# Two token steps of a 2048-point transform on 64 by 64 tiles of the PE array, and W fetched two groups at a time

## The chip, the cores and the metric

The kernel runs on one core of a Trainium2 chip. The metric is device time in microseconds. A profile is of one execution; its span runs from the first instruction to the last, and that execution's own time is a little longer. Engines are written as the profile writes them: PE (TensorE; PEld is its weight load), DVE (VectorE), ACT (ScalarE), POOL (GpSimd) and SP (SyncE, which only issues DMA transfers).

## What is computed

x is 2048 tokens by 1024 channels. Two branches read it, and a gate mixes them.

```
a = irfft2( rfft2(x) * (w_r + i w_i) )             # over tokens and channels; w: 2048 x 513
Lam_bar = exp(exp(log_dt) * Lambda)
B_bar   = ((Lam_bar - 1) / Lambda)[:, None] * (B_re + i B_im)
h[t]    = Lam_bar * h[t-1] + x[t] @ B_bar.T        # 1024 complex states, 2048 tokens in order
b       = 2 * Re(h @ (C_re + i C_im).T) + x * Dskip
g       = sigmoid(sum(x * gate_w, -1))
out     = g * a + (1 - g) * b
```

## The kernel before, in words

**The spectral branch (`gfnet`).** The 2048-point transform over tokens is split as 64 x 32. The first stretch, "the front", works in 16 row blocks j. `turn_x(j)` turns a block of x on PE (L684) and ACT copies it out (L685). `fold(j)` forms sums and differences on DVE (L695 to L701). `fd(j)` is the transform over channels, eight matmuls (L359, L362) copied to X1 by ACT or DVE (L365). `s1(j)` is the first token step with the twiddles T2: four matmuls of 64 rows each (L376), copied to A1 by DVE for j in 0, 1, 2, 3, 5, 6, 7, else by ACT (L381), then written to DRAM (L383). In the second stretch, 16 groups g of two rows b follow. `load(g)` brings Bb back turned (L408) and W, real and imaginary, each into both partition halves, in four transfers (L411). `s2(g)` is the second token step: two matmuls of 128x128 against the constant KRS (L488), which ACT copies to X2 (L490). `times_w(g)` makes the products X2 * w_i and X2 * w_r on DVE (L496, L497). The first inverse step, `ps_is1`, is four matmuls of 128x128 against the twiddles MT (L512, L513), copied to C1 by ACT (L515) and written to DRAM (L516). The third stretch reads that back turned (L530) and does the second inverse step in 16 blocks of sixteen 128x128 matmuls (L537), copied to ZT by ACT (L539). The inverse over channels is `spectral(tb)` (L629), per token tile.

Column 512 of W has no room in the half spectrum, so a small side path computes its products: `reverse_m`, `zps`, `qps` (L410 to L484). Its result Qn is put into column 0 of each X2 (L491).

**The state branch.** Tokens go in 8 chunks of 256. `unit(c, q)` makes the inputs of chunk c: two halves of 32 matmuls (L319), each copied to h by ACT (L321). `recur(c, ...)` then cuts the recurrence into DVE pieces: multiplications by a rotation table ("cross" and "along", L274, L277), joins (L280, L283), scans of 1024 columns each, four for a whole chunk (L289), a carry, and the rotation back. The table itself is made by `make_tab` in the front, in five parts per pair of blocks on DVE, ACT and POOL (L226 to L248, and L856 to L863). `early(tb)` is the output product of a token tile, two halves of 16 + 4 matmuls (L598, L602), for tiles 0 to 9; tiles 10 to 15 are done at the end. It waits for the pieces of its chunk. `load_C` and `load_xs` are DMA transposes (L583, L590) and write CT and xs.

**What sets the order.** The order on PE, DVE and ACT is that of the program (`manual_schedule`); the order on SP and POOL is chosen by the framework's own planner. In the front, `plan[j]` gives the order of turn (T), fold (f), `fd(j+1)` (F) and `s1(j)` (S); from j = 6 on the main loop places parts of the table, halves of the state branch and loads around it. `step()` advances the spectral branch by one stage, `halves(ssm, 1)` the state branch by one half. `vector(us)` takes DVE pieces off the list until their nominal costs reach the sum of the shares given so far; the shares are the numbers in SHARE, one per call. In the second stretch each group is: s2(g+2), ps_is1(g), times_w(g+1), loads for g+3, one half of the state branch, one share.

**Buffers that matter.** PSUM pool psA has two buffers, shared in turn by fd, s1, s2 and both inverse steps. Bb and W have three buffers each, V2 and C1 two. `raw` is 6144 columns wide: T2 takes its first half in the front, MT all of it in the second stretch, and the third stretch reads its blocks into it.

Of the kernel before, what the change touches and what calls it, by code (L numbers as in the profile page):

```python
# [32 lines left out]
    4, 5.2, 3.6, 5.9, 2.8, 1, 1, 2.2, 2.2, 3.7, 2.2, 3, 3, 3, 2.5, 3.5,  # L33
    3, 2.2, 3.3, 3.3, 4.8, 3.3, 3.3, 3.3, 3.3, 3.3, 3, 2.6, 3, 3.3, 3.3, 3.3,
    2.5, 3, 3.2, 3, 0, 2, 4, 2, 2, 2, 2.5, 2, 2, 1.5, 2, 2,
    2, 2, 2, 2, 3.5, 3.5, 3.5, 4, 6, 4, 4, 2, 4, 4, 4.5, 4.5,
    4.5, 4.5, 4.5, 4.8, 4.3, 4.3, 4.3,
# [8 lines left out]
def _host_consts():  # L46
# [14 lines left out]
    for cls in range(2):  # L61
        for kb in range(2):
# [10 lines left out]
    m1 = np.arange(64)[None, None, :]  # L73
# [20 lines left out]
    gr, gb, ga = f // 64, (f // 2) % 32, f % 2
    angR = 2 * np.pi * ((gb[:, None] * gb[None, :]) % 32) / 32
    R2 = (ga[:, None] == ga[None, :]) * np.where(gr[:, None] == gr[None, :], np.cos(angR),
                                                  np.where(gr[:, None] == 0, 1.0, -1.0) * np.sin(angR))
    R2 = R2.reshape(P, 64, 2).transpose(0, 2, 1).reshape(P, P)
    Sel = np.zeros((P, 2, 2, P))
    for h in range(2):  # L100
        for ri in range(2):
            Sel[2 * np.arange(64) + h, h, ri, 64 * ri + np.arange(64)] = 1.0
# [18 lines left out]
def kernel(  # L121
# [29 lines left out]
    W_v = [w.rearrange("(p b) k -> p b k", b=32) for w in (A_w_r, A_w_i)]  # L151
# [197 lines left out]
    def gfnet():  # L349
# [4 lines left out]
        def fd(j):  # L354
# [9 lines left out]
            X1 = gta.tile([P, 2, K], BF16, name="X1")  # L364
# [5 lines left out]
        def s1(j):  # L370
# [10 lines left out]
            (nc.vector.tensor_copy if j in (0, 1, 2, 3, 5, 6, 7) else nc.scalar.copy)(out=A1, in_=psa)  # L381
# [14 lines left out]
        MT_sb = raw.rearrange("p (b n) -> p b n", n=192)  # L396
# [5 lines left out]
        t1_v = turn1_dram.rearrange("j (r a b) k -> (j r a) b k", r=2, a=2)  # L402
        Wb = fft["Wb"]

        def load(g):
            bs = slice(2 * g, 2 * g + 2)
            Bb = gt.tile([P, 2, K], BF16, name="Bb", tag="gin", bufs=3)
            nc.sync.dma_start(out=Bb, in_=t1_v[:, bs])  # L408
            for w in range(2):
                for r in range(2):  # L410
                    nc.sync.dma_start(out=Wb[g % 3][64 * r:64 * (r + 1), w, :, 1:K], in_=W_v[w][:, bs, 1:K])  # L411
            return Bb

# [22 lines left out]
        loads = [load(0), load(1), load(2)]  # L436
# [4 lines left out]
        nc.vector.tensor_copy(out=Bcol[:, 0:2].rearrange("j c a b -> j (c a b)"), in_=aps)  # L441
# [64 lines left out]
        for g in range(16):  # L506
# [13 lines left out]
            if g + 3 < 16:  # L520
                loads.append(load(g + 3))
# [343 lines left out]
    for _ in range(5):  # L865
        front()
# [145 lines left out]
```

## Time and profile before

| | before |
|---|---|
| median of 3 runs | 339.19 us (338.52 to 339.42) |
| the profiled execution: time | 338.71 us |
| the profiled execution: span | 336.9 us |
| mean granted PE clock | 0.995 |
| PE, DVE, ACT, POOL busy | 323.7, 286.7, 169.3, 32.4 us |
| moved by DMA | 58.45 MB, 173 GB/s over the span |

In rows of the timeline a group of neighbouring equal instructions is one line: start, length, engine, line of the code, operation, output <- inputs, shapes and count; in square brackets stands the idle time of the engine before it and what ended that. A matmul's length reaches past the start of the next one, so PE work is read from start to start. SPq rows are the issuing of transfers, not the transfers.

### The profile page before, as it was taken

Reading aid. Unit: us, or ns where it says so; the run is one execution under the profiler, and the core shown is the slowest. Engines: PE = TensorE matmul, PEld = TensorE weight load, DVE = VectorE, ACT = ScalarE, POOL = GpSimd, SP = SyncE. Lnnn points to the kernel's source line nnn. Section 1 sums busy time; section 2 is a strip of 40 time slices with the busy share of each in tenths; the row PEclk is TensorE's granted clock in tenths of the full one; section 3 lists DMA queues with packets and bytes.
Section 4 is the critical chain, followed back from the end, with each engine's and each line's share of the span. In section 5 each row is a group of like instructions: output and inputs, shape, how many; then the busy total and the mean of one; then the engine's idle time right before and its main releaser. Section 6 shows DMA issues by size and latency. Waiting matters only on the chain.

```text
span 336.9 us, 6192 instructions
## 1 busy us (share of the span) xinstructions
PE 323.7 (96%) x2446; PEld 213.7 (63%) x2446; DVE 286.7 (85%) x403; ACT 169.3 (50%) x213; POOL 32.4 (10%) x64
## 2 busy tenths in 40 slices
PE   8998859999999999999999999999999999999995
PEld 4564636676885675747566576869845876565552
DVE  2798895899979789999999999899680999999951
ACT  3888679746351155647556551646632243443510
POOL 1481112020000000000000000000000002211220
PEclk9999989999999999999999999999999999999999
DMA  7999999999992447889999956997214003776594
GB/s 265 378 175 227 204 211 208 164 172 218 272 220 55 115 135 175 251 192 284 261 253 252 232 163 170 216 195 203 70 28 136 19 0 53 109 159 89 98 156 154
DMA packets 83581, 58.45 MB, mean 173 GB/s; under 512 B 54328, under 2 KB 74304, under 8 KB 83424
## 3 DMA queue, kind: packets, MB, share of 16 engines
q1 hardware_dynamic: 80304, 55.38, 66.8%
q0 software_dynamic: 3168, 2.66, 8.7%
q8 instruction: 19, 0.31, 0.4%
q14 instruction: 10, 0.08, 0.1%
q10 hardware_dynamic: 80, 0.01, 0.0%
HBM read 30.23 MB, written 17.83 MB: 143 GB/s over the span
## 4 chain that ended last, share of the span: by engine, by line
PE 83%; ACT 5%; DVE 5%; SPq 4%; issue 1%; DMA 1%; ACTq 0%; DVEq 0%
PE ps_y L598 29%; PE psu L319 28%; PE ps_h L598 4%; PE ps_id L629 4%; SPq L583 3%; PE ps_fd L359 2%; PE ps_is L537 2%; PE ps_is L513 2%; PE ps_is L512 2%; PE ps_s L488 2%; PE ps_y L602 2%; PE pt L684 2%; PE psw L710 1%; ACT xQ L685 1%; SPq L411 1%
## 5 line engine op out<-in xcount | busy, mean ns | idle before, releaser
L319 PE MATMUL psu<-xQ,BT 128*128 128x256 bf16 x1024 | 117.9, 275 | 0.8 <-ACT ye L616 0.5
L319 PEld LDWEIGHTS <-BT 128*128 128x128 bf16 x1024 | 100.1, 99 | 17.4 <-issue 3.2
L598 PE MATMUL ps_y<-CT,h 128*128 128x512 bf16 x448 | 101.3, 379 | 0.0
L598 PEld LDWEIGHTS <-h 128*128 128x128 bf16 x512 | 49.4, 98 | 55.4
L289 DVE TENSOR_TENSOR_SCAN h<-rz,h 128x1024 bf16<-128x1024 f32 x32 | 71.5, 2274 | 0.1
L321 ACT CAST h<-psu 128x1024 bf16<-128x1024 f32 x32 | 32.3, 1010 | 52.5 <-PE psu L319 49.2
L277 DVE TENSOR_TENSOR h<-h,tab 128x4096 bf16<-128x4096 bf16 (+1 forms) x20 | 37.3, 1863 | 0.7
L644 POOL DMA_DIRECT2D BT<-y_scratch x10 | 11.9, 1194 | 235.4 <-DVE BT L638 235.1
L616 ACT ACTIVATE ye<-ps_y,omg 128x512 f32<-128x512 f32 x20 | 12.7, 684 | 43.4 <-PE ps_y L602 35.7
L274 DVE TENSOR_TENSOR xQ<-h,tab 128x4096 bf16<-128x4096 bf16 x12 | 27.4, 2287 | 4.4 <-ACT h L321 4.3
L490 ACT CAST X<-ps_s 128x1024 bf16<-128x1024 f32 x16 | 16.2, 1014 | 8.7 <-PE ps_s L488 8.7
L359 PE MATMUL ps_fd<-G_sb,preT 128*128 128x512 bf16 x64 | 16.5, 380 | 1.2 <-ACT X L365 1.2
L685 ACT COPY xQ<-pt 128x1024 bf16<-128x1024 bf16 x16 | 15.4, 1024 | 2.5 <-PE pt L684 2.5
L539 ACT CAST ZT<-ps_is 128x1024 bf16<-128x1024 f32 x16 | 15.5, 1023 | 2.2 <-PE ps_is L537 2.2
L695 DVE TENSOR_TENSOR preT<-xQ 128x512 bf16<-128x512 bf16 x16 | 7.3, 453 | 10.9 <-ACT xQ L685 7.6
L515 ACT CAST C<-ps_is 128x1024 bf16<-128x1024 f32 x16 | 16.1, 1008 | 0.0
L629 PE MATMUL ps_id<-raw,ZT 128*128 128x256 bf16 x128 | 15.9, 273 | 0.0
L365 ACT CAST X<-ps_fd 128x1024 bf16<-128x1024 f32 x14 | 14.2, 1013 | 3.0 <-PE ps_fd L362 2.9
L376 PE MATMUL ps_s<-X,raw 64*128 64x512 bf16 x64 | 9.7, 380 | 5.1 <-DVE CT L381 4.5
L598 PE MATMUL ps_h<-CT,h 128*128 128x512 bf16 x64 | 14.5, 379 | 0.0
L629 PEld LDWEIGHTS <-ZT 128*128 128x128 bf16 x128 | 12.4, 98 | 2.2
L496 DVE TENSOR_TENSOR V<-X,Wb 128x1024 bf16<-128x1024 bf16 x16 | 10.9, 680 | 1.6 <-issue 1.5
(194 smaller groups left out, 367.9 us busy)
## 6 DMA issues: line engine op xcount, KB each, us to landing
y_scratch<-ye SPq DMA_DIRECT2D x20, 256.0 KB, 2.6
CT<-in_A_x_dram SPq DMA_DIRECT2D x8, 512.0 KB, 5.4
Bb<-turn_scratch SPq DMA_DIRECT2D x16, 256.0 KB, 4.0
turn_scratch<-C SPq DMA_DIRECT2D x16, 256.0 KB, 5.1
raw<-turn_scratch SPq DMA_DIRECT2D x16, 256.0 KB, 4.5
Wb<-in_A_w_r_dram SPq DMA_DIRECT2D x32, 127.8 KB, 4.1
Wb<-in_A_w_i_dram SPq DMA_DIRECT2D x32, 127.8 KB, 3.8
out_dram<-BT SPq DMA_DIRECT2D x14, 256.0 KB, 5.2
```

The source lines that it names most:

```text
L274: nc.vector.tensor_mul(out=tmps["s"], in0=u[:, ::-1], in1=bc(i))
L277: nc.vector.tensor_mul(out=u, in0=u, in1=bc(i))
L289: nc.vector.tensor_tensor_scan(out=seg, data0=rz[:, js.start + j:js.start + j + 4].rearrange("p j t -> p (j t)"), data1=seg, initial=0.0, ...
L319: nc.tensor.matmul(psu[:, j, :], lhsT=BT[4 * q + j][:, ri, d8, :], rhs=xQ[:, c, d8, :], start=(d8 == 0), stop=(d8 == 7))
L321: nc.scalar.copy(out=hs[c][:, ri, 4 * q:4 * q + 4].rearrange("p b (q j) -> p b q j", j=32), in_=psu.rearrange("p b (j q) -> p b q j", j=32))
L359: nc.tensor.matmul(ps[:, 1, :], lhsT=preTs[j][:, 4 + d4, :], rhs=Go[:, d4, :], start=(d4 == 0), stop=(d4 == 3))
L490: nc.scalar.copy(out=X2, in_=ps2)
L515: nc.scalar.copy(out=C1.rearrange("p h (c i) -> p h c i", c=2), in_=psc.rearrange("p h (i c) -> p h c i", c=2))
L539: nc.scalar.copy(out=ZT[:, 4 * kp:4 * kp + 4, :, 8 * G:8 * G + 8].rearrange("p (c r) n t -> p c r n t", c=2), in_=psz.rearrange("p c (t r ...
L598: nc.tensor.matmul(psy, lhsT=hs[c][:, ri, jb, P * tq:P * (tq + 1)], rhs=CT[ri][:, jb, 512 * dh:512 * (dh + 1)], start=(i == 0), stop=False)
L629: nc.tensor.matmul(pse[:, slot, :], lhsT=ZT_t[:, i, tb, :], rhs=fft["Gi"][:, i, :], start=(kb == 0), stop=(kb == 1))
L685: nc.scalar.copy(out=x_gjq[:, :, :, :, j, :].rearrange("p c d g q -> p d c g q"), in_=pt.rearrange("p d (c q g) -> p d c g q", c=NCH, g=2))
```

## The change

**The tiles.** The frequency order that s1 leaves, and all constants behind it, are permuted so that the second token step couples 64 rows with 64 rows: KRS's first part becomes two copies of a 64 x 64 matrix, and the twiddles MT need 96 columns a row instead of 192. `s2(g)` is then four matmuls of 64x64x512 with `tile_position` (64b, 64c), and `ps_is1(g)` eight, in two rounds that add up in PSUM. The row half of a tile goes with the PSUM bank it writes. The inverse over tokens is thereby split 32 then 64, before 64 then 32; the second inverse step keeps its number and size of matmuls, and its block of input comes in one transfer instead of two. The matmuls of `qps` are four of 32 columns instead of four of 16, and Qn is made by four copies instead of one.

**The fetch.** W sits in two double buffers, each for two groups, one of them partly in the half of `raw` that MT no longer takes. `load_W(i)` brings one of w_r and w_i for two groups in four transfers of 32 partitions by 4 rows. Each partition quarter takes the rows that its 32 frequencies need. Bb has a fourth buffer, also in `raw`. Four groups are loaded ahead instead of three, and each turn of the loop asks for group g+4.

**The order.** `plan` and the loops that stood around it are replaced by one string, ORDER, one letter per act: T, f, F, S as above, h a half of the state branch, v a share, t a part of the table, a a part of the small vectors, b one load of B, c one load of C, s a step of the spectral branch, x the change of PSUM pools, and so on (`acts`). X1 has four buffers instead of two. The A1 copies of s1(2) go to ACT, those of s1(4) and s1(15) to DVE. Written in one notation (S8 is s1(8), u01a the first half of unit(0,1), t4 the fifth part of the tables), the part of the front around s1(8) is

```
before: t0 f10 F7 S6 b b t1 t2 u00a t3 t4 f11 f12 F8 S7 b b t5 t6 u00b t7 t8 F9 f13 S8
after:  t0 f10 F7 b t1 t2 S6 b t3 t4 f11 u00a f12 F8 t5 b b S7 u00b t6 t7 F9 t8 f13 S8
```

The order of halves and of spectral stages in the second and third stretch is the same as before; shares fall at other places and have other sizes. The diff, without most of the constants and without the moved small-vector lines:

```diff
 SHARE = (
-    4, 5.2, 3.6, 5.9, 2.8, 1, 1, 2.2, 2.2, 3.7, 2.2, 3, 3, 3, 2.5, 3.5,
-    3, 2.2, 3.3, 3.3, 4.8, 3.3, 3.3, 3.3, 3.3, 3.3, 3, 2.6, 3, 3.3, 3.3, 3.3,
-    2.5, 3, 3.2, 3, 0, 2, 4, 2, 2, 2, 2.5, 2, 2, 1.5, 2, 2,
-    2, 2, 2, 2, 3.5, 3.5, 3.5, 4, 6, 4, 4, 2, 4, 4, 4.5, 4.5,
-    4.5, 4.5, 4.5, 4.8, 4.3, 4.3, 4.3,
+    4.9, 4.3, 2.1, 5.9, 1.3, 2.5, 3.5, 0.6, 2.5, 4, 2.5, 4.2, 1.5, 3, 2.5, 3.5,
+    4.3, 2.2, 3.3, 2.3, 4.8, 3.3, 2.3, 3.3, 5.3, 1.7, 3, 3.2, 3, 2.7, 2.3, 1.8,
+    2.9, 3, 5.3, 4, 0, 3.5, 4, 1, 2, 2, 3.6, 2.4, 1.4, 3, 0.8, 0.2,
+    2, 2, 3.5, 1.7, 3.8, 6, 3.2, 2.5, 4.5, 4, 3.7, 2.3, 4.3, 4.3, 5.7, 3.7,
+    3.9, 4.5, 2.7, 8.4, 5.8, 4.3, 4,
+)
+ORDER = (
+    "TFfSTfTFTfTbbSbbFTTfSTTbFbfTfSTbbwFTTfb2STbfFaSabbxaatfFbttSbttf",
+    "hfFtbbShttFtfSthSttthfFtttvFSktttthtvgfFSttchvtFStctthFvScttttth",
+    "tvFtStttvtcSvtt|cccsvhcvhvhdvehshvshvhvvshhvshvsshvsshvsshvsshvs",
+    "shvsshsshvvsshvsshvsshvsshvsshsvshvsshvsshvsshvsshvhvhvsvshvsvsh",
+    "vsvshvsshvvsvshsvshvsvivshvsvshv",
 )
 
...
+    K2 = cs(f % 2, h // 32, 2 * np.pi * (((f // 2) * (h % 32)) % 32) / 32)
+    K2 = np.concatenate([K2, K2], axis=1)
+    angM = 2 * np.pi * (((64 * (f % 32) + 32 * (f // 64) + gb) * np.arange(32)[None, None, :]) % S) / S
+    Mre = np.where((f // 32) % 2 == 0, np.cos(angM), -np.sin(angM))
+    Mim = np.where((f // 32) % 2 == 0, np.sin(angM), np.cos(angM))
...
-    W_v = [w.rearrange("(p b) k -> p b k", b=32) for w in (A_w_r, A_w_i)]
+    W_v = [w.rearrange("(m c b) k -> c m b k", c=2, b=32) for w in (A_w_r, A_w_i)]
...
-            X1 = gta.tile([P, 2, K], BF16, name="X1")
+            X1 = gta.tile([P, 2, K], BF16, name="X1", bufs=4)
...
-            (nc.vector.tensor_copy if j in (0, 1, 2, 3, 5, 6, 7) else nc.scalar.copy)(out=A1, in_=psa)
+            (nc.vector.tensor_copy if j in (0, 1, 3, 4, 5, 6, 7, 15) else nc.scalar.copy)(out=A1, in_=psa)
...
-        MT_sb = raw.rearrange("p (b n) -> p b n", n=192)
+        MT_sb = raw[:, 0:3 * D].rearrange("p (b n) -> p b n", n=96)
...
-        t1_v = turn1_dram.rearrange("j (r a b) k -> (j r a) b k", r=2, a=2)
+        t1_v = turn1_dram.rearrange("j (r g b c) k -> g b (j r) c k", r=2, g=16, b=2)
         Wb = fft["Wb"]
 
         def load(g):
-            bs = slice(2 * g, 2 * g + 2)
-            Bb = gt.tile([P, 2, K], BF16, name="Bb", tag="gin", bufs=3)
-            nc.sync.dma_start(out=Bb, in_=t1_v[:, bs])
-            for w in range(2):
-                for r in range(2):
-                    nc.sync.dma_start(out=Wb[g % 3][64 * r:64 * (r + 1), w, :, 1:K], in_=W_v[w][:, bs, 1:K])
+            Bb = (gt.tile([P, 2, K], BF16, name="Bb", tag="gin", bufs=3) if g % 4 < 3
+                  else raw[:, 5 * D:6 * D].rearrange("p (c k) -> p c k", c=2))
+            nc.sync.dma_start(out=Bb, in_=t1_v[g])
             return Bb
+
+        def load_W(i):
+            pair, w = i // 2, i % 2
+            for q in range(4):
+                nc.sync.dma_start(out=Wb[pair % 2][w][32 * q:32 * (q + 1), :, 1:K], in_=W_v[w][q // 2][:, 4 * pair:4 * pair + 4, 1:K])
...
-        loads = [load(0), load(1), load(2)]
+        loads = [load(g) for g in range(4)]
+        for i in range(4):
+            load_W(i)
...
-        qps = psA.tile([P, 2, 16], FP32, name="qps", tag="ps")
-        for h in range(2):
-            for ri in range(2):
-                nc.tensor.matmul(qps[:, h, :], lhsT=fft["Sel"][:, 2 * h + ri, :], rhs=Qb[:, :, ri],
-                                 start=(ri == 0), stop=(ri == 1))
+        qps = psA.tile([P, 4, 32], FP32, name="qps", tag="ps")
+        for a4 in range(4):
+            nc.tensor.matmul(qps[:, a4, :], lhsT=fft["Sel"][:, a4, :], rhs=Qb.rearrange("p b r -> p (b r)"), start=True, stop=True)
         Qn = fx.tile([P, 2, 16], BF16, name="Qn")
-        nc.vector.tensor_copy(out=Qn, in_=qps)
-        Qn = Qn.rearrange("p h b -> p (h b)")
+        for q in range(4):
+            at = slice(32 * q, 32 * (q + 1))
+            nc.vector.tensor_copy(out=Qn[at], in_=qps[at, 2 * (q // 2):2 * (q // 2) + 2, q % 2:32:2])
+        Qn = Qn.rearrange("p a b -> p (a b)")
 
         def s2(g):
             ps2 = psA.tile([P, 2, K], FP32, name="ps_s2", tag="ps")
-            for h in range(2):
-                nc.tensor.matmul(ps2[:, h, :], lhsT=KRS_sb[:, 0, :], rhs=loads[g][:, h, :], start=True, stop=True)
+            for b in range(2):
+                for c in range(2):
+                    nc.tensor.matmul(ps2[64 * c:64 * (c + 1), b, :], lhsT=KRS_sb[64 * b:64 * (b + 1), 0, 0:64],
+                                     rhs=loads[g][64 * b:64 * (b + 1), c, :], start=True, stop=True, tile_position=(64 * b, 64 * c))
...
-            nc.vector.tensor_mul(out=V2, in0=X2, in1=Wb[g % 3][:, 1])
-            nc.vector.tensor_mul(out=X2, in0=X2, in1=Wb[g % 3][:, 0])
+            nc.vector.tensor_mul(out=V2, in0=X2, in1=Wb[g // 2 % 2][1][:, 2 * (g % 2):2 * (g % 2) + 2])
+            nc.vector.tensor_mul(out=X2, in0=X2, in1=Wb[g // 2 % 2][0][:, 2 * (g % 2):2 * (g % 2) + 2])
...
             psc = psA.tile([P, 2, K], FP32, name="ps_is1", tag="ps")
-            for h in range(2):
-                b = 2 * g + h
-                nc.tensor.matmul(psc[:, h, :], lhsT=MT_sb[:, b, 64:192], rhs=UV[0][:, h, :], start=True, stop=False)
-                nc.tensor.matmul(psc[:, h, :], lhsT=MT_sb[:, b, 0:128], rhs=UV[1][:, h, :], start=False, stop=True)
+            for u, n in ((0, 32), (1, 0)):
+                for b in range(2):
+                    for c in range(2):
+                        rows = slice(64 * c, 64 * (c + 1))
+                        nc.tensor.matmul(psc[64 * b:64 * (b + 1), c, :], lhsT=MT_sb[rows, 2 * g + b, n:n + 64], rhs=UV[u][rows, b, :],
+                                         start=(u == 0), stop=(u == 1), tile_position=(64 * c, 64 * b))
...
-            if g + 3 < 16:
-                loads.append(load(g + 3))
+            if g + 4 < 16:
+                loads.append(load(g + 4))
+                load_W(g + 4)
...
-        ZT = fft["ZT"].rearrange("p i t (h u) -> p i (t h) u", h=2)
-        t2_v = turn2_dram.rearrange("b (r G a g) k -> G r b a g k", r=2, a=2, g=4)
+        ZT = fft["ZT"].rearrange("p i t (h u) -> p i (t h) u", h=4)
+        t2_v = turn2_dram.rearrange("b (y G g) k -> G (b y) g k", y=4, g=4)
 
         for G in range(8):
             Cq = raw[:, 2 * D * (G % 3):2 * D * (G % 3 + 1)].rearrange("p (g k) -> p g k", g=4)
-            for r in range(2):
-                nc.sync.dma_start(out=Cq[64 * r:64 * (r + 1)], in_=t2_v[G, r])
+            nc.sync.dma_start(out=Cq, in_=t2_v[G])
             for kp in range(2):
                 psz = psA.tile([P, 2, K], FP32, name="ps_is2", tag="ps")
                 for kl in range(2):
                     kc = 2 * kp + kl
-                    pv = psz[:, kl, :].rearrange("p (a g n) -> p a g n", a=2, g=4)
                     for g in range(4):
-                        nc.tensor.matmul(pv[:, :, g, :], lhsT=Cq[:, g, P * kc:P * (kc + 1)], rhs=KRS_sb[:, 1, :],
+                        nc.tensor.matmul(psz[:, kl, P * g:P * (g + 1)], lhsT=Cq[:, g, P * kc:P * (kc + 1)], rhs=KRS_sb[:, 1, :],
                                          start=True, stop=True)
-                nc.scalar.copy(out=ZT[:, 4 * kp:4 * kp + 4, :, 8 * G:8 * G + 8].rearrange("p (c r) n t -> p c r n t", c=2),
-                               in_=psz.rearrange("p c (t r n) -> p c r n t", t=8, r=2))
+                nc.scalar.copy(out=ZT[:, 4 * kp:4 * kp + 4, :, 4 * G:4 * G + 4].rearrange("p (c r) n g -> p c r n g", c=2),
+                               in_=psz.rearrange("p c (g r n) -> p c r n g", g=4, r=2))
...
-        fft["Wb"] = [fft["wp"].tile([P, 2, 2, K], BF16, name=f"Wb{i}") for i in range(3)]
+        halves_of_W = [fft["wp"].tile([P, 4, K], BF16, name=f"Wb{i}") for i in range(3)]
+        halves_of_W.append(raw[:, 3 * D:5 * D].rearrange("p (x k) -> p x k", k=K))
+        fft["Wb"] = [halves_of_W[0:2], halves_of_W[2:4]]
...
+    def small():
+        nc.vector.tensor_copy(out=ang2[:, 0], in_=thp)
+        nc.vector.tensor_scalar_mul(out=ang2[:, 1], in0=thp, scalar1=float(TC))
+        yield from sincos(sp, ang2, [P, 2, 8], s2c, c2c, "a2")
...
+    def turn(r):
+        turn_x(r)
+        turns_left[0] -= 1
+
+    def use_psU():
+        assert not turns_left[0]
+        xctx.close()
+        pools["u"] = ctx.enter_context(tc.tile_pool(name="psU", bufs=2, space=PSUM, reuse_waits="tile"))
+
+    def front_done():
+        for _ in tables:
+            pass
+        tctx.close()
+
+    def make_dgD():
+        nc.vector.tensor_mul(out=fft["dgD"], in0=ident.unsqueeze(1).to_broadcast([P, 8, P]),
+                             in1=vecT[:, 3].unsqueeze(2).to_broadcast([P, 8, P]))
+
+    acts = {
+        "T": in_turn(turn, 2), "f": in_turn(fold, 2), "F": in_turn(fft["fd"], 1), "S": in_turn(fft["s1"], 0),
+        "h": lambda: halves(ssm, 1), "v": lambda: vector(next(share)), "t": lambda: next(tables, None),
+        "a": lambda: next(smalls, None), "x": use_psU, "g": gate, "b": lambda: load_B(1), "c": in_turn(lambda q: load_C(q - 8), 8),
+        "2": lambda: load_T2(8, 16), "w": load_Wcols, "k": load_small, "|": front_done,
+        "s": step, "d": make_dgD, "e": gate_end, "i": after_ic,
+    }
+    for act in "".join(ORDER):
+        acts[act]()
```

## The prediction, made before the change was run

> **What bounds the kernel now.** I read, in this order, the page's busy shares, the table by stage, the PE timeline of the stage that the change rebuilds, the PE timeline of the front, and then the DVE and SP timelines beside both.
>
> ```profile
> PE 323.7 (96%) x2446; PEld 213.7 (63%) x2446; DVE 286.7 (85%) x403; ACT 169.3 (50%) x213; POOL 32.4 (10%) x64
> ...
> 31.30:52.70 21.40, 16.88 (x127) 12.07 (x128) 19.18 (x59) 15.09 (x27) 3.90 (x6) 0.92 1.11 220
> ...
> 122.70:200.80 78.10, 78.10 (x514) 48.78 (x513) 75.51 (x70) 45.55 (x64) 0.00 (x0) 1.00 0.90 229
> ```
>
> The columns of the last two are the stretch, its length, then PE, PEld, DVE, ACT and POOL busy, the granted clock, the DMA share and GB/s. PE is idle for only 13.2 us of the 336.9 us span. From 122.7 to 200.8 (second token step and first inverse step, with SSM work between the groups) it is never idle, so every PE microsecond taken out there shortens the span until another engine takes over. DVE is the candidate: 75.5 of 78.1.
>
> ```profile
> 137.03 0.59 PE L488 MATMUL ps_s<-Bb,KRS_sb 128*128 128x512 bf16 x2
> 137.47 0.38 PE L512 MATMUL ps_is<-X,raw 128*128 128x512 bf16 x1
> 137.68 0.38 PE L513 MATMUL ps_is<-V,raw 128*128 128x512 bf16 x1
> ...
> 138.33 3.66 PE L319 MATMUL psu<-xQ,BT 128*128 128x256 bf16 x32
> ```
>
> This is one of 16 groups on PE. Read starts, not durations, because matmuls overlap: a 512-column matmul starts 0.215 us after the one before, and the six take 137.03 to 138.33, **1.30 us**.
>
> **Step 1, the blocks.** In the change a group has twelve matmuls of 64 rows by 64 columns, four at a time on disjoint quarters of the array. Does PE run such tiles together? Two nearest rows:
>
> ```profile
> 30.77 0.60 PE L362 MATMUL ps_fd<-G_sb,preT 128*128 128x256 bf16 x4
> 31.31 0.61 PE L376 MATMUL ps_s<-X,raw 64*128 64x512 bf16 x4
> 31.85 3.67 PE L319 MATMUL psu<-xQ,BT 128*128 128x256 bf16 x32
> ...
> 59.93 3.66 PE L319 MATMUL psu<-xQ,BT 128*128 128x256 bf16 x32
> 63.52 1.91 PE L737 MATMUL zps_g<-xQ,gw 128*32 128x512 bf16 x32
> 65.36 1.04 PE L359 MATMUL ps_fd<-G_sb,preT 128*128 128x512 bf16 x4
> ```
>
> L376 splits the rows in two: four matmuls take 0.54 us, where full ones take 0.86. That is 2 x 0.215 + 0.11; and L362 before it takes 0.54 instead of the 0.44 it takes ahead of a full matmul. So the tiles run in pairs, and a visit to the tiled form costs about 0.2 us. L737 splits the columns in four, each with a stream of its own: 32 matmuls in 1.84 us = 8 x 0.215 + 0.12, and the psu ahead of it takes 3.59 instead of 3.50. Again four at once and 0.2 per visit. Rows and columns split together do not occur in this trace. I take the same rule: 3 x 0.215 + 0.2 = 0.845 us a group, saving 0.455. Bounds: 0.755 if one half of the switch is hidden; 1.57 if each matmul with its load needs 114 ns (twice the 57 ns of an L737 pair, for twice its columns).
> Groups 0 to 13: 14 x 0.455 = 6.4. The first two s2 alone: 0.87 becomes 0.63, 0.24. Groups 14 and 15 have no s2: 0.87 and 0.86 become 0.63, 0.47. Sum **7.1 us off PE**. The later inverse step keeps its 128 matmuls of 128x128 (0.89 us a block): nothing.
>
> The weight side: L448 gets through 16 load-and-matmul pairs in 0.49 us, 31 ns each, with 128 columns; the new tiles load 64 columns, 12 loads against 0.645 us of streaming, so up to 54 ns each is hidden. [...]
>
> **Step 2, does DVE let it through?** PE's stage becomes 71.0 us; DVE has 75.5. The new SHARE numbers release less scan work here. Adding the released pieces at their rows (n=8: cross and along 2.30, scan 2.21, joins 1.14 to 1.4), I get 50.1 us between the first and last inverse block before and 46.7 after. DVE then has 72.1 for 71.0. Margins in the trace: the W products are done 1.4 us (the sixth, ending 155.58 for PE at 156.99) to 5 us before PE takes them, and DVE idled 1.55 at the stage's start. Walking product by product with 0.845, I find all in time but two, 0.2 late each: **+0.4**. What is deferred finds DVE idle from 240 to 261 (3.16 and 9.56 us).
>
> **Step 3, SP and the fetch of W.** The change issues as many W transfers a group as before (four, 128 KB), only shaped 32 partitions x 4 rows. So nothing is saved per group; but four groups rather than three are fetched ahead, and Bb has four buffers.
>
> ```profile
> 185.02 1.32 SPq L411 DMA_DIRECT2D Wb<-in_A_w_r_dram  x2
> 186.39 1.84 SPq L411 DMA_DIRECT2D Wb<-in_A_w_i_dram  x2
> ...
> 193.68 0.68 DVE L496 TENSOR_TENSOR V<-X,Wb 128x1024 bf16<-128x1024 bf16 x1
> ```
>
> The last W is issued by 188.2, lands 4 us later (median), and is used at 193.68: 1.5 us of margin. From 123 to 194 SP issues for 61.9 of 71.4 us, and from 161.2 with no gap over 0.1: it is nearly a second bound. After: 48 W issues in the stage instead of 52, 12 Bb instead of 13, each 0.6 with 0.07 between; with writes and transposes some 54 us up to the last W, for a last need 63 us after the first s2. Starting at 7 and adding 4 of landing, that is 0.5 late: **+0.5** (bounds 0 and 4, below). Queue order on SP is the scheduler's; three places have cover. Five more loads ahead of the first group cost 3 us of SP before xs (issued to 93.5, landing 3.7, used 103.4). One C load moves behind them in the code (used by the second early half, 104.2): if it went behind the Bb loads (to 99.7) it would end at 99.7 + 2.6 + 4.6 = 106.9, 2.7 late; I take 0. The raw reads of the second inverse step become 8 issues instead of 16 and have 1.2 us of margin before 211.66: 0.
>
> **Step 4, the front.** Its PE order around the worst stall is the same.
>
> ```profile
> 41.97 1.03 PE L359 MATMUL ps_fd<-G_sb,preT 128*128 128x512 bf16 x4
> 42.84 0.60 PE L362 MATMUL ps_fd<-G_sb,preT 128*128 128x256 bf16 x4
> 46.84 0.61 PE L376 MATMUL ps_s<-X,raw 64*128 64x512 bf16 x4 [3.40 <-DVE CT L381]
> 47.38 5.33 PE L319 MATMUL psu<-xQ,BT 128*128 128x256 bf16 x32
> ```
>
> PE waits 3.40 us for a PSUM buffer that DVE copies out behind table and fold work; then 32 matmuls take 5.27 us to the next start, not 3.50, and the clock column of that stretch says 0.77: **1.77 us** for a lowered clock. In the new ORDER the t2 products of the table (L242) go to ACT ahead of the copy of h (L321); now they wait behind it and DVE waits 0.79 for them (40.00). That wait goes: **-0.8**, gap 2.6. Does the clock hold then? Rows: after gaps of 1.22 and 1.12 it stayed, after 3.40 it fell. 2.6 is nearer the latter, but nothing in between is shown; I take that it holds, **-1.8** (bounds 0 and -1.8). [...] The stalls of 1.22 (29.91), 1.12 (37.93), 0.62 and 0.40 (84 to 85) have the same releasers in the new order: 0. Moving copies (S2 to ACT; S4 and S15 to DVE) is even in sum; S15's bank is not wanted until 99.8. Four small Qn copies instead of one (0.18 each) lie in DVE's 1.55 us gap.
>
> **Sum.** -7.1 + 0.4 + 0.5 - 0.8 - 1.8 = -8.8. The profiled execution took 338.71 (span 336.9 and 1.8 around it): **329.9 us**. It is 0.48 under the median shown, 339.19; so read a gain of 8.8 us, 2.6%.
>
> **Rivals.**
> 1. The clock still drops after 2.6 us: 331.7. For it: 2.6 lies nearer 3.40. Chance 0.18.
> 2. SP takes over. Its last four groups begin 4.95 us apart (165.22 to 185.02), PE's wish is 4.4. Held for ten groups that loses 5.5, less the 1.5 of margin: 4.0 instead of 0.5, so 333.4. For it: no gap from 161. Against: one group fewer to fetch. 0.17.
> 3. **Slower.** Weight loads of the 64x64 tiles run one by one and set the pace. At 91 ns a pair a block costs 1.30 and gains nothing; from about 103 ns the front's 2.6 is used up too. At 114: 14 x 0.27 + 0.24 + 0.48 = +4.5, with the front 340.6 (waits of steps 2 and 3 gone). Against: 31 and 57 ns pairs. Were the four tiles not concurrent at all, a block would take 12 x 0.215 + 0.2 = 2.78 and the time be near 360. Together 0.09.
> 4. Loads partly exposed: a 64-column pair at 62 ns, between the rows of 31 and 114 and just over L737's 57, makes a block 12 x 0.062 + 0.2 = 0.94, 0.1 more for each of 16: 331.5. 0.10. [...]
> 5. Better: half the switch hidden (0.755, 1.4 more) and the early ACT waits (1.22 and 0.48) also gone: 326.8. 0.08.
> The forecast itself: 0.38.
>
> **How the numbers follow.** Cases 1, 2, 4 and the forecast hold 0.83; their ends with the open terms (C load +2.7 on 331.7; hidden switch -1.4 on 329.9) give 328.5 to 334.4, and I widen to 327.5 and 335.0 for half of case 5 and a smaller part of the late W in case 2. About 0.3% (1 us) is what a measurement of this kernel can tell from no change. Faster 0.88: all but case 3 and a 0.03 slice in which case 2 and a late C load meet; slower 0.09; same 0.03.
>
> **What would show it.** Step 1: start of the s2 tiles to the next full matmul 0.8 to 0.9 us, and no more than 1.3. Step 2: no PE wait on DVE L496/L497 over 0.3. Step 3: few DVE waits on W transfers. Step 4: a gap near 2.6 before the ninth s1, and the next psu at 3.5. A block over 1.3 us, or a stage from first s2 to last inverse block longer than 75 us instead of 71.5, makes this wrong.

## The result, and the profile after

The changed kernel takes **396.89 us** (median of 4 runs, 394.76 to 398.16) against 338.86 for the kernel before beside it: ratio 1.170, 95% interval 1.165 to 1.176. The forecast was 329.9. The profiled execution took 396.43 us, its span 394.6, 57.7 more than before. The PE timeline says where:

| kernel | median, lowest to highest, us | ratio to before (95%) | to Wrev | to first s2 | stage | rest |
|---|---|---|---|---|---|---|
| before | 338.86, 338.52-339.42 | 1 | 85.3 | 37.4 | 78.3 | 135.9 |
| after | 396.89, 394.76-398.16 | 1.170 (1.165-1.176) | 86.1 | 51.6 | 120.9 | 136.1 |
| e1 Bb by halves | 338.63, 334.49-340.79 | 0.997 (0.994-0.999) | 83.7 | 37.5 | 75.4 | 136.0 |
| e2 before, Bb with 2 entries outermost | 396.86, 395.45-400.31 | 1.173 (1.169-1.177) | 85.2 | 46.6 | 127.7 | 135.9 |
| e18 before, 4 entries outermost | 358.32, 357.65-359.10 | 1.057 (1.054-1.060) | 86.0 | 37.4 | 98.0 | 136.0 |
| e3 e1, full array | 341.23, 336.00-343.74 | 1.000 (0.997-1.003) | 85.4 | 37.4 | 79.4 | 135.9 |
| e4 e1, old order | 336.41, 335.90-341.43 | 0.994 (0.992-0.996) | 85.4 | 37.5 | 78.1 | 136.1 |
| e6 e1, half of Bb on POOL | 338.97, 335.86-345.34 | 0.992 (0.990-0.993) | 85.3 | 37.5 | 75.1 | 136.3 |
| e7 e1, half of Bb on ACT | 342.28, 336.65-346.27 | 1.005 (1.002-1.008) | 87.7 | 39.9 | 80.7 | 136.1 |
| e9 e7, full array | 343.14, 341.32-347.45 | 1.012 (1.009-1.015) | 83.9 | 37.4 | 82.8 | 136.0 |
| e8 e1, front and A1 writes | 345.29, 344.08-345.44 | 1.018 (1.017-1.020) | 94.3 | 37.5 | 75.8 | 136.1 |
| e11 e1, Bb asked earlier | 334.45, 332.18-338.70 | 0.986 (0.982-0.990) | 84.5 | 37.5 | 76.4 | 136.0 |
| e12 e11 and front | 336.31, 333.40-338.63 | 0.992 (0.989-0.995) | 83.8 | 40.2 | 76.5 | 136.1 |
| e13 e11, full array | 339.41, 336.23-341.99 | 0.998 (0.996-1.001) | 86.1 | 39.9 | 78.2 | 136.0 |
| **e14** e12 and A1 buffers | 333.37, 331.76-334.85 | 0.984 (0.981-0.987) | 83.3 | 37.5 | 74.1 | 136.1 |
| e15 e14, half of W's bytes | 329.86, 328.92-330.31 | 0.973 (0.971-0.975) | 82.4 | 37.6 | 72.4 | 136.1 |
| e16 e14, full array | 335.94, 335.29-337.00 | 0.992 (0.990-0.993) | 81.9 | 37.4 | 78.2 | 135.9 |

The last four columns are stretches of the profiled execution on PE: from the start to the first matmul of Wrev (the side path's, L422 in the changed kernel), from there to the first s2, from there to the end of the last inverse block (the stage of 16 groups), and the rest. Medians count every execution; the ratios leave out those over 1.5% above the fastest of their kernel, so the two need not agree to the last tenth. The ratios of e1 to e18 are against runs of before taken beside each (medians 338.65 to 338.70).

After loses 14.2 us between Wrev and s2 and 42.6 us in the stage; the rest is 0.8 and 0.2. The table by stage, and a group of the stage on the PE timeline:

```profile
PE 335.8 (85%) x2542; PEld 212.8 (54%) x2542; DVE 289.4 (73%) x407; ACT 169.3 (43%) x212; POOL 32.5 (8%) x62
```

```profile
86.07:137.60 51.53, 41.05 (x325) 28.53 (x325) 36.59 (x73) 9.09 (x11) 0.00 (x0) 0.87 0.68 128
137.60:258.50 120.90, 87.06 (x610) 47.34 (x610) 71.11 (x65) 46.26 (x64) 0.00 (x0) 0.86 0.67 141
```

```profile
141.66 0.39 PE L614 MATMUL ps_y<-dgD,xs 128*128 128x128 bf16 x4
141.97 0.41 PE L496 MATMUL ps_s<-Bb,KRS_sb 64*64 64x512 bf16 x4
142.21 0.39 PE L523 MATMUL ps_is<-X,raw 64*64 64x512 bf16 x4
142.43 0.39 PE L523 MATMUL ps_is<-V,raw 64*64 64x512 bf16 x4
142.75 3.63 PE L610 MATMUL ps_y<-CT,h 128*128 128x512 bf16 x16
```

The tiles do what was forecast: 141.97 to 142.75 is 0.78 us, and the operation ahead of them takes 0.31 instead of 0.23. But PE, without an idle microsecond in this stage before, now idles for 34 of 121 us, its clock is 0.86, and the DMA share and GB/s have *fallen* (0.90 to 0.67, 229 to 141). Less moved, and everyone waiting for it: the list of waits (engine, line, releaser: total, times, longest) and the DMA view of 100 to 125 us, in 40 slices of 0.625 us, show how:

```profile
DVE V L505 <- DMA Wb<-in_A_w_i_dram: 27.4, 3, 11.4
...
PE ps_s L496 <- DMA Bb<-turn_scratch: 18.8, 6, 5.3
...
PE ps_y L614 <- DMA xs<-in_A_x_dram: 10.5, 1, 10.5
...
PE ps_s L496 <- DMA raw<-turn_scratch: 10.3, 3, 3.5
```

```profile
DMA  9251211111111111111111111991111111111999
GB/s 183 39 92 46 52 46 52 52 52 52 46 52 52 49 49 49 52 49 49 49 49 49 52 49 61 207 72 49 52 49 49 49 49 49 52 49 40 230 290 369
```

```profile
103.00:109.00 6.00, 6.00 (x45) 3.04 (x44) 5.80 (x12) 0.32 (x1) 0.00 (x0) 1.00 0.13 51
```

```profile
99.08 3.02 SPq L410 DMA_DIRECT2D Bb<-turn_scratch  x3
102.14 7.41 SPq L410 DMA_DIRECT2D raw<-turn_scratch  x1
109.59 13.64 SPq L602 DMA_TRANSPOSE xs<-in_A_x_dram  x2
```

Four Bb (one of them in raw), 1 MB, are nearly all that is out. For some 20 us the DMA engines are one tenth busy and move 50 GB/s, and SP, in order, stays 7 and 14 us in the issues behind. The row by stage from 103 to 109 us gives the tenth as 0.13, which is what two of sixteen engines at work would show (2/16 = 0.125), at 25 GB/s each.

### The profile page after: what moved, and what is told of

Its sections match the earlier page's. It is cut to its first block, busy times and chain, and to the rows that moved or that the text cites. A ratio compares the mean times of both kernels' runs of the same rounds, so it can differ in the third digit from the quotient of the medians.

```text
span 394.6 us, 6347 instructions
## 1 busy us (share of the span) xinstructions
PE 335.8 (85%) x2542; PEld 212.8 (54%) x2542; DVE 289.4 (73%) x407; ACT 169.3 (43%) x212; POOL 32.5 (8%) x62
## 4 chain that ended last, share of the span: by engine, by line
PE 57%; DMA 23%; DVE 9%; SPq 4%; ACT 4%; issue 2%; ACTq 0%; DVEq 0%
PE psu L321 20%; PE ps_y L610 18%; DMA Bb<-turn_scratch 8%; DMA xs<-in_A_x_dram 4%; PE ps_h L610 4%; DMA Wb<-in_A_w_r_dram 3%; DMA raw<-turn_scratch 3%; PE ps_id L641 3%; DMA turn_scratch<-C 3%; PE ps_fd L361 3%; SPq L410 3%; PE ps_is L547 2%; PE ps_fd L364 1%; PE ps_s L378 1%; PE ps_y L614 1%
## 5 line engine op out<-in xcount | busy, mean ns | idle before, releaser
L321 PE MATMUL psu<-xQ,BT 128*128 128x256 bf16 x1024 | 124.1, 283 | 0.8 <-ACT ye L628 0.5
L321 PEld LDWEIGHTS <-BT 128*128 128x128 bf16 x1024 | 102.3, 102 | 23.9 <-issue 9.0
L610 PE MATMUL ps_y<-CT,h 128*128 128x512 bf16 x448 | 109.4, 401 | 0.0
L610 PEld LDWEIGHTS <-h 128*128 128x128 bf16 x512 | 50.7, 102 | 64.1 <-issue 15.5
L505 DVE TENSOR_TENSOR V<-X,Wb 128x1024 bf16<-128x1024 bf16 x8 | 5.5, 688 | 27.6 <-DMA Wb<-in_A_w_i_dram 27.4
L496 PE MATMUL ps_s<-Bb,KRS_sb 64*64 64x512 bf16 x48 | 5.3, 446 | 18.8 <-DMA Bb<-turn_scratch 18.8
L505 DVE TENSOR_TENSOR V<-X,raw 128x1024 bf16<-128x1024 bf16 x8 | 5.5, 683 | 21.2 <-PE ps_is L523 17.2
L496 PEld LDWEIGHTS <-KRS_sb 64*64 64x64 bf16 x64 | 1.8, 107 | 32.0 <-DMA Bb<-turn_scratch 20.2
L614 PE MATMUL ps_y<-dgD,xs 128*128 128x128 bf16 x88 | 8.7, 223 | 10.5 <-DMA xs<-in_A_x_dram 10.5
L614 PEld LDWEIGHTS <-xs 128*128 128x128 bf16 x88 | 6.8, 99 | 15.9 <-DMA xs<-in_A_x_dram 11.0
```

The source lines that it names most:

```text
L321: nc.tensor.matmul(psu[:, j, :], lhsT=BT[4 * q + j][:, ri, d8, :], rhs=xQ[:, c, d8, :], start=(d8 == 0), stop=(d8 == 7))
L610: nc.tensor.matmul(psy, lhsT=hs[c][:, ri, jb, P * tq:P * (tq + 1)], rhs=CT[ri][:, jb, 512 * dh:512 * (dh + 1)], start=(i == 0), stop=False)
L614: nc.tensor.matmul(psy[:, P * d4:P * (d4 + 1)], lhsT=xs[tb][:, d8, :], rhs=fft["dgD"][:, d8, :], start=False, stop=(d4 == 3 and ga is None))
```

## The experiments

**Theory 1:** Bb's new pattern `"j (r g b c) k -> g b (j r) c k"` has b, of size 2, outermost, and the transfer is carried by as many engines as that. **Rivals:** W's fetch in 32 partitions by 4 rows, or SP's longer queue (2); the tiles or the new order (3).

**e1, Bb in halves.**

```diff
-            nc.sync.dma_start(out=Bb, in_=t1_v[g])
+            for b in range(2):
+                nc.sync.dma_start(out=Bb[64 * b:64 * (b + 1)], in_=t1_v[g, b])
```

> The changed kernel with one edit: each Bb comes by two transfers of 64 partitions, one for each value of b, so that each transfer's outermost dimension is j with 32 rows and not b with 2; bytes, buffers, tiles, W's fetch and the order stay. Theory 1 (a transfer whose outermost dimension has 2 entries is carried by 2 of the 16 DMA engines, about 25 GB/s each): the waits on Bb, on raw (which holds every fourth Bb) and on Wb behind them go; the stretch from Wrev to the first s2 falls from 51.6 to 36 to 40 us, the stage of 16 groups from 120.8 to 70 to 74 us, the whole to 329 to 336 us. Theory 2 (W's fetch in transfers of 32 partitions by 4 rows is what is slow, or SP's longer queue of issues): the waits stay, and the whole is above 375 us. Theory 3 (the tiles or the new order carry part of it): between, 345 to 375 us.

Measured: Wrev to s2 37.5, stage 75.4, 338.63 us (the profiled execution 334.49). Theory 1 holds, the slow transfers are gone with W and the queue as they were; but neither the stage (70 to 74) nor the whole (329 to 336) is the expected one, and its executions spread over 6 us, those of before over 2.6.

**e2 and e18, the pattern alone, in the kernel before.** Nothing of the change is in them but the order of Bb's rows (K2's rows follow):

```diff
-        t1_v = turn1_dram.rearrange("j (r a b) k -> (j r a) b k", r=2, a=2)
+        t1_v = turn1_dram.rearrange("j (r a b) k -> a (j r) b k", r=2, a=2)     # e2: 2 outermost
+        t1_v = turn1_dram.rearrange("j (r a b) k -> (r a) j b k", r=2, a=2)     # e18: 4 outermost
```

> The kernel before with one edit: the rows of Bb are put in the order (a, j, r) instead of (j, r, a), so that its one transfer's outermost dimension has 2 entries instead of 32; the constant K2 has its rows permuted to match, the result is the same, and everything else is that of before. Theory 1: the two engines that carry Bb have 128 KB of it each a group, and a sixteenth of W (32 KB) and of C1 (8 KB): about 168 KB at 25 GB/s, 6.7 us a group against the 4.9 us that a group took; so 16 times 1.8 us more, and up to 10 us before the first s2: 365 to 395 us. Theory 2 (W's new shape or the longer queue): 338 to 341 us, as before.

> The kernel before with the rows of Bb in the order (r, a, j), so that the outermost dimension of its one transfer has 4 entries instead of 32 (K2's rows permuted to match, same result). In e2, with 2 entries, the stage took 127.7 us, 8 us a group. If 4 entries mean 4 engines at about 25 GB/s each, the Bb of a group takes 2.6 us there instead of 5.2, and these engines have 64 KB of Bb, 32 KB of W and about 8 KB of C a group, 104 KB or 4.2 us against the 4.9 us that a group takes: a loss of 0 to 8 us, 339 to 347 us. If the loss does not follow the number (a pattern that is slow by its order of rows, whatever the number), 380 us and more, as in e2.

Measured: e2 396.86 us, the whole loss of the change without the change. e18 358.32. The DMA view from 93 to 131 us, slices of 0.95 us, first e2, then e18:

```profile
DMA  9998449100111111199111111499600000099500
GB/s 324 319 209 127 17 89 261 31 2 32 50 52 52 52 50 52 50 126 100 50 50 50 50 50 50 97 287 393 235 0 0 0 0 0 14 256 351 207 0 0
```

```profile
DMA  8896931149222226209960000079800000123678
GB/s 323 343 262 114 301 49 53 76 137 165 103 101 99 101 96 131 42 6 244 346 233 6 11 0 0 0 150 344 334 0 0 0 0 0 32 60 106 182 188 170
```

50 GB/s at one tenth with two entries, 100 at two tenths with four: 25 an entry. That bears theory 1 out, and rivals 2 and 3 are not needed for the loss. My sum for the price was low both times (365 to 395 and 339 to 347 us expected, from the bytes on the busiest engines, 6.7 and 4.2 us a group; the stage took 8.0 and 6.1): what else holds those engines is open. Two and four of sixteen engines would show shares of 0.125 and 0.25, and the digits of these stretches are one and two tenths; which engines moved Bb no view says.

**e3 and e4, tiles and order on top of e1.** e3 writes s2 and is1 as full matmuls, two and four a group; e4 spells the old plan and shares in the new letters.

> The kernel of e1 with the second token step and the first inverse step as full 128 by 128 matmuls (two for the step s2 and four for is1, as before had them, on the operands that are there: these two steps so compute other numbers). It prices the tiles where they stand. If a tiled block takes about 0.87 us and a full one 1.30 us, and PE is what a group waits for, e3 is 5 to 8 us slower than e1. If PE is no longer what a group waits for (DVE's products or the transfers are), e3 is within 2 us of e1.

> The kernel of e1 with the order of before written out in the new letters (ORDER and SHARE; tiles, buffers and fetches stay). It prices the new order. As forecast (the shorter gap before s1(8), and the clock that holds behind it) e4 would be 1 to 3 us slower than e1. If the new order gains nothing in the front (its mark at Wrev came 0.8 us later than in the kernel before), e4 is 0 to 2 us faster than e1. If the later part of the new order is what lets loads and products keep up with the shorter blocks, e4 is more than 4 us slower, with the difference in the stage of 16 groups.

Measured: e3's stage is 4.0 us longer than e1's, its median 2.6, and by the ratios the whole differs by 1.1 us: under the 5 to 8 that PE alone would give, so something other than PE holds e1. e4 is 2.2 us faster by the median (0.9 by the ratios), though its profiled stage is 2.7 us longer, 1.7 of it in a fall of the clock behind a wait of 2.17 us on Bb. No gain from the new order shows, and the scatter of e1 hides more than that.

**Why e1 is not 330: who bounds the stage now.**

```profile
121.20:196.70 75.50, 72.11 (x607) 43.18 (x610) 69.94 (x65) 45.63 (x64) 0.00 (x0) 1.00 0.89 225
```

PE has 72 us of work in 75.5, and its waits are on Bb(9) and Bb(13). SP's and PE's rows around the first:

```profile
151.02 0.85 SPq L630 DMA_DIRECT2D y_scratch<-ye  x2
151.97 0.39 SPq L528 DMA_DIRECT2D turn_scratch<-C  x1
152.44 1.76 SPq L411 DMA_DIRECT2D Bb<-turn_scratch  x2
```

```profile
157.81 0.94 PE L497 MATMUL ps_s<-Bb,KRS_sb 64*64 64x512 bf16 x4 [0.99 <-DMA Bb<-turn_scratch]
```

The buffer of Bb(9) is free from 139.5 (s2(5)), but its issue stands behind the write of C, which waits for ACT. I first put it down to the number of SP's issues, and moved the second half of each Bb from group 4 on to ACT (e7, and e9 with full matmuls) or POOL (e6): `(nc.scalar if b and g > 3 else nc.sync).dma_start(...)`, and `nc.gpsimd` in e6.

> The kernel of e1, with the second half of each Bb from group 4 on issued by ACT instead of SP. In the profile of e1 the stage took 75.4 us and not 71, PE waited three times on Bb for 2.7 us, and SP issued from 142 to 187 us with hardly a gap: about 3.5 us a group for C, Bb and W, and more for y and xs. Theory A (SP's issuing is the bound of the stage once the tiles have shortened it): 12 issues of 0.55 us leave SP, the waits on Bb go, the stage takes 71 to 72.5 us, and the whole falls by 2 to 4 us against e1. Theory B (DVE's products are the bound): the stage stays at 74 to 75.5 us and PE waits on V and X instead. Theory C (the bytes are the bound, the DMA engines being 90% busy): the waits on Bb stay.

> The kernel of e3 (both steps as full 128 by 128 matmuls; these two steps so compute other numbers) with the same half of Bb issued by ACT. Its stage is bound by PE, so under theory A it gains little: stage 78 to 79 us, 6 to 8 us above that of the kernel with tiles and the same issuing. Under B or C the difference of the two stages stays at 3 to 5 us.

> As e7, but with the second half of each Bb from group 4 on issued by POOL, which stands idle in this stage. Theory A: as e7, stage 71 to 72.5 us. If POOL's way of issuing is slower (its transfers of 256 KB took 5.3 us from issue to landing, SP's 3.7 to 3.9), the loads still have a group's time in hand and the result is the same. Theory B or C: 74 to 75.5 us.

Measured: stage 80.7 (e7), 82.8 (e9) and 75.1 (e6); PE's waits on Bb 6.0 us in e7, 3.0 in e6. Theory A falls with e6: 6.6 us of issuing taken off SP left the stage where it was. From ACT it was worse by the ratios, with tiles (1.005 against 0.997) and without (1.012 against 1.000); why is open. How much worse the stage of e7 does not say, since its profiled execution, 346.27 us, is the longest of its twelve.

**e11, Bb asked for earlier; e13 the same with full matmuls.** `load(g + 4)` moves from the end of group g to ahead of `ps_is1(g)`; on SP it then stands before the write of C(g).

> The kernel of e1, with Bb for group g+4 asked for before the inverse blocks of group g instead of behind them; its buffer is free by then. In the profile of e1 the three waits on Bb fall on Bb(9) and Bb(13), whose issue (152.4, 171.7 us) stands on SP directly behind the write of C, which waits for ACT's copy of that group; with half of Bb on another queue the other half still stood there and the waits stayed. Theory A (the place in SP's order makes Bb late): the waits on Bb fall from 2.7 us to under 0.5, the stage from 75.4 to 72 to 73 us, the median 2 to 3 us below that of e1. Theory B (the number of SP's issues, or the bytes): W or C now come late instead, the stage stays within 1 us of 75.4.

> The kernel of e11 with both steps as full 128 by 128 matmuls, as in e3 (these two steps so compute other numbers). If nothing but PE bounds the stage once Bb comes in time, the difference of the two stages is the 6 to 7.1 us that the blocks differ by, against the 4.0 us between e3 and e1; if DVE or SP holds the kernel with tiles, it stays at 4 to 5.

Measured: 334.45 us, 4.2 below e1's median (3.6 by the ratios). The wait on Bb(9) went, one of 1.8 on Bb(13) stayed, and behind it the clock fell (below), so the profiled stage is 76.4. Neither theory: order mattered, and something is left. The difference to e13's stage can't be read for the same reason: 1.8 us as it stands, some 3.5 with the 1.7 of the fall taken out of e11's.

**e15 and e16, bytes or issues.** e14 (below) with W's transfers cut to half their columns from the third pair on, issues unchanged: `N = K if i < 4 else K // 2`. e16 is e14 with full matmuls.

> The kernel of e14 with W's transfers from the third pair of groups on cut to the first half of their columns (the other half keeps older values: this computes other products), at the same number of transfers and issues. Theory A (bytes: the DMA engines are full in the stage): the wait on Bb(13) of 1.8 us and the DVE waits on W (3.1 us) go, the stage falls from 74.1 to 71 to 72.5 us, the whole by 1.5 to 3 us. Theory B (SP's issues or their order): the waits stay, within 0.7 us of e14.

> The kernel of e14 with both steps as full 128 by 128 matmuls (these two steps so compute other numbers). Its stage is bound by PE at 78.2 us; that of e14 took 74.1 with one wait of 1.8 us in it. So 3.5 to 5 us slower than e14, 337 to 338.5 us. If the executions of e14 owe nothing to the tiles, the same as e14.

The stage in the table by stage, e14, e15, e16:

```profile
120.80:195.00 74.20, 71.83 (x606) 43.06 (x610) 69.59 (x65) 45.59 (x64) 0.00 (x0) 1.00 0.96 229
```

```profile
119.90:192.40 72.50, 71.92 (x611) 43.04 (x610) 69.77 (x65) 45.50 (x64) 0.00 (x0) 1.00 0.69 190
```

```profile
119.30:197.60 78.30, 78.30 (x515) 48.85 (x514) 70.55 (x65) 45.73 (x64) 0.00 (x0) 1.00 0.90 219
```

Read the last two columns with the first. With full matmuls PE sets 78.3 us and the DMA engines are 0.90 busy. The tiles want the same bytes in 72, and at 0.96 of the engines they come late: 74.2. With half of W the share is 0.69, the wait on Bb(13) falls from 1.8 to 0.6 and the stage is 72.5 at the same number of issues. As a whole e15 is 3.5 us below e14 by the medians, where 1.5 to 3 was expected. Bytes, then, not issues: the tiles are worth 78.2 - 72.4 = 5.8 us of stage, 6.4 without that last 0.6, and the DMA engines let 4.1 of it through (e16 to e14). The whole shows less, 2.6 us (medians 335.94 and 333.37), below the 3.5 to 5 expected: in the front of e14's profiled execution the clock fell at s1(10), 1.1 us net, and in those of e15 and e16 it held (rows in the last section).

**e8, e12, e14, the front.** e8: in ORDER f11 and f12 go behind S7, and the A1 writes of j = 10 to 14 are issued by ACT. e12: e11 with the first of these edits alone. e14: e12 with six A1 buffers instead of four, X1 back to two.

```diff
-  ... F7 b t1 t2 S6 b t3 t4 f11 u00a f12 F8 t5 b b S7 u00b ...
+  ... F7 b t1 t2 S6 b t3 t4 u00a F8 t5 b b S7 f11 f12 u00b ...                  # e8, e12, e14
-            nc.sync.dma_start(out=t1_w[j], in_=A1)
+            (nc.scalar if 10 <= j < 15 else nc.sync).dma_start(out=t1_w[j], in_=A1)    # e8
-    A1_4 = gta.tile([P, 4, 2, K], BF16, name="A1", bufs=1)
+    A1_4 = gta.tile([P, 6, 2, K], BF16, name="A1", bufs=1)                      # e14
```

The first two lines are in the notation of the orders in the section on the change. The diff leaves out that e8 starts from e1 and the other two from e11, and e14's indices into A1 and its `bufs=2` for X1.

> The kernel of e1 with two edits in the front: in ORDER the folds 11 and 12 come behind s1(7) instead of before it, so that DVE copies s1(7) out about 2.5 us earlier; and the writes of A1 for j = 10 to 14 are issued by ACT instead of SP, where they stood behind transposes of C. If the gap of 2.1 us before s1(8) and the lowered clock that follows it in some executions have that one cause: the gap falls under 1 us, the next psu takes 3.5 us in every execution, and the executions lie within 1.5 us of each other instead of 4.5. If the wait at Wrev (1.0 to 2.7 us) comes from those writes, it falls to about 0.4. Together 2 to 4 us less than e1's median, 334.5 to 336.5 us. If the wait only moves to another s1, no change.

> The kernel of e11 with folds 11 and 12 behind s1(7) in ORDER, as in e8, but with the writes of A1 left on SP (in e8 the first of them, on ACT, waited 9.6 us for transposes, which cost that kernel its time). The gap of 2.1 us before s1(8) should vanish, as it did in e8, a gap of about 1.9 us remain before s1(10), and the next psu take 3.5 us in every execution if it is the long gap that lowers the clock. Then the front ends 0 to 1 us earlier than e11's in an execution whose clock held and about 2 us earlier than in one whose clock fell; the median of e12 is 0.5 to 2 us below e11's. If a gap of 1.9 us lowers the clock too, no change.

> The kernel of e12 with six buffers for A1 of j = 8 to 15 instead of four, and X1 back to two of the four, which pay for it; the copy of A1(14) then waits for the write of A1(8) and not of A1(10), which stands on SP behind transposes of C. The wait at Wrev (1.0 to 2.7 us) should fall to about 0.4 and the median by 0.6 to 2 us against e12. If the wait comes from elsewhere, no change; if X1's buffers were needed, waits of PE on X1 appear in the front.

e8 lost its time at one place, ACT's rows:

```profile
60.63 1.00 ACT L383 CAST A<-ps_s 128x1024 bf16<-128x1024 f32 x1
70.79 0.42 ACTq L385 DMA_DIRECT2D turn_scratch<-A  x1
71.26 1.01 ACT L323 CAST h<-psu 128x1024 bf16<-128x1024 f32 x1 [9.62 <-DMA CT<-in_B_C_re_dram]
```

The first write from ACT stood for 9.6 us until transposes of C, issued by SP, had landed, and ACT's copies behind it, and PE behind those (9.2 us before s1(11)). What ties that write to the transposes is open. The fold edit did its part in all three: no wait before s1(8), but 1.9 us before s1(10), where ACT's copy of X1 is late; the wait moved, as the expectation's last case said. e12 is not faster than e11 (336.31 to 334.45), against the 0.5 to 2 us expected. e14's wait at Wrev is 0.4 (e12: 2.3, with the clock falling behind it), and 333.37 is the best of the versions that compute the whole result: 1.6% faster than before (1.3 to 1.9).

**e17, e1 once more, for the clock.**

> One more execution of e1 with its profile. In the first its gap before s1(8) was 2.11 us and the clock held behind it (psu 3.6 us from start to start); the executions of after, e3 and e11 had the same gap and a psu of 5.27 us. If a gap of 2.1 us lowers the clock in some executions only, this one shows either, with the front 1.6 us apart between the two; a clock that depends on the kernel would give 3.6 again.

341.66 us; to Wrev 85.8 (a wait of 3.6 there), Wrev to s2 40.2, stage 77.8. The gap before s1(8) was 2.12 and the clock held again, which a clock that depends on the kernel would give too; this run does not tell the two apart.

## Why the prediction was wrong, by its steps

**Step 3 failed, and it is the step that decided.** It says "The change issues as many W transfers a group as before" and "So nothing is saved per group", and prices Bb at a row of before, 0.6 us of SP each. It counted issues and bytes and took the duration of a transfer along from the old pattern to a new one. The pattern was in the diff; with two entries outermost Bb moves at 50 GB/s, and that alone, put into the kernel before, costs 58 us (e2), as much as the change lost. No rival had it: rival 2 saw the fetch as SP's issuing, and rival 3, the slower side, looked at the weight loads.

Its second term was too small as well. With Bb mended, "+0.5" for the late fetch is some 2.3 us (e14's stage 74.1 against 71.8 without waits), and through the DMA engines' bytes, not SP. The row of before that said so was shown in the prediction: DMA share 0.90 over the stage. A tenth less time at equal bytes had to fill them.

What is left with both mended shows in e14: its span is 5.9 us shorter than that of before, 4.2 in the stage (the forecast's steps 1 to 3 give 6.2) and 2.0 up to Wrev (forecast 2.6, and here by the other edits of e14), less 0.3 elsewhere.

**Step 1 was right.** 0.78 and 0.09 make a block of 0.87 (forecast 0.845); ahead of it psu takes 3.60 instead of 3.49. Worth 6.4 us of the 7.1. No run shows rival 4's 62 ns a pair; its block of 0.94 did not come, one of 0.87 did.

**Step 2 was right.** In e15 PE waits for DVE nowhere in the stage, in e11 once for 0.32 us, where 0.4 was forecast.

**Step 4 was half right.** The 0.79 us wait went and the gap fell, to 2.11 and not 2.6. "I take that it holds", with no row of before between gaps of 1.22 and 3.40 us to go by, failed in after. The same gap at the same place, before s1(8), in after and in e1:

```profile
45.31 0.61 PE L378 MATMUL ps_s<-X,raw 64*128 64x512 bf16 x4 [2.11 <-DVE CT L383]
45.85 5.33 PE L321 MATMUL psu<-xQ,BT 128*128 128x256 bf16 x32
51.12 0.60 PE L378 MATMUL ps_s<-X,raw 64*128 64x512 bf16 x4
```

```profile
45.36 0.61 PE L378 MATMUL ps_s<-X,raw 64*128 64x512 bf16 x4 [2.11 <-DVE CT L383]
45.90 3.67 PE L321 MATMUL psu<-xQ,BT 128*128 128x256 bf16 x32
49.50 0.61 PE L378 MATMUL ps_s<-X,raw 64*128 64x512 bf16 x4
```

From start to start 5.27 and 3.60. Of nine profiled executions with this gap the clock fell in five (after, e3, e6, e9, e11) and held in four (e1, e7, e13, e17). So a gap of 2.11 us did not settle the 1.8 us for the clock: it was lost in five of nine, where rival 1 had given that 0.18. The loss that step 4 did not see at all came at Wrev: a wait of 0.4 to 3.6 us on a copy whose buffer's write stood on SP behind transposes of C; 2.69 in after. Six A1 buffers took it away in e14.

## What to carry to other kernels

When a change turns a transfer's access pattern, read its outermost dimension before its bytes. Here Bb moved 50 GB/s at one tenth of the DMA engines with 2 entries outermost (e2) and 100 at two tenths with 4 (e18), and in after SP's issues behind the first three Bb stood for 7.4 and 13.6 us. The sign in the profile was a low DMA share with few GB/s (0.13 and 51 in after) while Bb and what stood behind it were waited for, and the test is to put that pattern alone into the old kernel. And before shortening a stage by a faster engine, look at the DMA share of that stage: at 0.90, as here, the bytes were the next bound, 74.1 us of stage (e14) where PE had 71.8 of work.

## What the runs showed of the hardware that was not expected

The clock fell after single PE waits as short as 1.81 us (e11), and not always for the same wait. Besides the nine above: after single waits of 1.5 to 1.7 us it always held (in e2 it fell behind one of 1.73, but that stood shortly after one of 2.91); before s1(10), after 1.86 or 1.87 us, it held in e8, e12, e15 and e16 and fell in e14; after a wait on Bb(13) it fell in e4 (2.17), e12 (1.86), e17 (1.83) and e11 (1.81) and held in e8 (1.83), e14 (1.77) and e6 (1.71). First s1(10) in e14 (56.25 to 61.51, 5.26 us for 32 matmuls; in e15 they took 3.67 and a wait of 0.54 followed), then Bb(13) in e11 and e14:

```profile
55.71 0.61 PE L378 MATMUL ps_s<-X,raw 64*128 64x512 bf16 x4 [1.87 <-ACT X L367]
56.25 5.33 PE L321 MATMUL psu<-xQ,BT 128*128 128x256 bf16 x32
61.51 1.91 PE L753 MATMUL zps_g<-xQ,gw 128*32 128x512 bf16 x32
```

```profile
178.02 0.93 PE L497 MATMUL ps_s<-Bb,KRS_sb 64*64 64x512 bf16 x4 [1.81 <-DMA Bb<-turn_scratch]
...
179.55 5.07 PE L612 MATMUL ps_y<-CT,h 128*128 128x512 bf16 x15 [0.17 <-issue]
```

```profile
176.22 0.86 PE L499 MATMUL ps_s<-Bb,KRS_sb 64*64 64x512 bf16 x4 [1.77 <-DMA Bb<-turn_scratch]
...
177.67 3.40 PE L614 MATMUL ps_y<-CT,h 128*128 128x512 bf16 x15 [0.16 <-issue]
```

Waits of 2.28 (e12), 3.34 (e13), 3.50 (e7) and 3.60 us (e17) at Wrev cost 2.4 to 2.7 us each between Wrev and s2; 1.98 (e1) cost nothing. Longer waits have held as well: 2.32 and 2.65 us in e18, 2.60 in e2, and 3.19 in after, where the 32 matmuls behind it run at full speed:

```profile
184.61 0.41 PE L496 MATMUL ps_s<-Bb,KRS_sb 64*64 64x512 bf16 x4 [3.19 <-DMA Bb<-turn_scratch]
...
185.38 3.67 PE L321 MATMUL psu<-xQ,BT 128*128 128x256 bf16 x32
```

So in these executions, between 1.8 and 3.2 us, the length of the wait does not decide, and the falls that can be priced cost 1.1 us (s1(10) in e14, where a wait went with it) to 2.7. That it differs from execution to execution of one kernel, no place profiled twice shows (e1 and e17 agree at s1(8)), but the mean granted clocks point to it: e14's six executions have 0.990 to 1.000, e12's ten 0.983 (338.63 us) to 1.000 (333.40). What else decides is not in these traces.
